# Batch 3's queries and keys by way of DRAM and transposing DMAs, in a fused attention and maxout FFN kernel

## The chip, the cores and the metric

One core of a Trainium2 chip runs the whole program. The metric is the device time of one execution in microseconds; lower is better. The profile's engines are PE (TensorE matmul), PEld (its weight loads), DVE (VectorE), ACT (ScalarE), POOL (GpSimd) and SP (SyncE, which here only issues DMAs).

## The reference

Causal attention over 8 batches of 8 heads, 576 positions, head size 64, with 16 extra "beacon" keys and values ahead of each head's own, followed by a feed-forward layer with three input matrices and a maximum. Shapes: q, k, v are 8 x 8 x 576 x 64 in float32, the beacons 8 x 8 x 16 x 64, the input matrices 512 x 768, the output matrix 768 x 512, the output 4608 x 512.

```python
k_all = concat([beacon_k, k], axis=2); v_all = concat([beacon_v, v], axis=2)
scores = (1 / sqrt(D)) * q @ k_all.T            # a query sees all beacons
scores = where(causal, -1e9, scores)            # and the keys up to its own
a = softmax(scores)
x = (a @ v_all) with the heads side by side      # 4608 tokens x 512
h = max(max(x @ w1, x @ w2), x @ w3)
out = h @ w_out
```

## The kernel before

**The work.** The kernel goes over 32 pairs of heads, four pairs to a batch (`PPB`), in order. For pair p it needs the queries and keys in bf16 with the head dimension on the partitions: one of four tiles `qT` and one of four tiles `kT` (`NT = 4`, so pair p uses the tiles that pair p - 4 used). A burst (`emit_burst`, L505, matmuls at L496) makes the scores of the pair and ACT turns them into exponentials (L514); POOL zeroes what the causal mask hides (`emit_masks`, L536). After every second pair, the products with the values follow (`emit_pv_whole`, L594, matmuls at L613) for the two pairs before, and ACT and DVE normalise them into `xT`. Between bursts PE does the feed-forward layer of earlier tokens: units of matmuls at L689 (input matrices) and L737 (output matrix), which DVE and ACT empty from PSUM (L707, L709, L744).

**The order.** It is written out by hand; each engine takes its instructions in program order. Batches 0 and 1 have functions of their own. From pair 8 on, `emit_all` (L1016) runs one step per pair. Step p is: the burst of pair p; if p is even, the products of pairs p - 2 and p - 1; the masks of pair p; some 4 to 6 units of the feed-forward layer; and the jobs of a plan, kept under (p, 0) and (p, 1). The jobs of (p, 0) come after the step's second unit, those of (p, 1) at its end. In this document "step p" is that turn of the loop.

**How queries and keys reach `qT` and `kT`.** Every pair is loaded in float32 from its input into one of eight `st` tiles (`load_pair`, L217, DMAs at L224) and cast to bf16 by POOL (`cast_pair`, L268, casts at L262, one for q and one for k). From there two ways are in use:

- Batches 1 to 3 (pairs 4 to 15): `turn_pair` (L439) makes 12 transposing matmuls of 96 x 96 on PE (L389) into two PSUM banks; DVE copies out the keys (L434) and ACT the queries (L423, by DVE for four pairs); `place_beacons` (L428) puts the beacon keys ahead of the keys by a small ACT copy (L430). In the main loop the turn of pair p + 1 stands behind the first unit of step p.
- Batches 4 to 7 (pairs 16 to 31): `store_pair` (L370) writes the cast pair to a DRAM tensor by two DMAs (L374), `fetch_pair` (L379) reads it back by two transposing DMAs straight into `qT` and `kT` (L381, L382). `open_dram` (L361) first puts the batch's beacon keys into that tensor (L365), out of `bk16`, which POOL casts once for all four batches (the cast that the profile shows at L811) from `bk32`, loaded by `load_beacons` (L336). For pair p these three jobs stand in the plan at steps p - 5, p - 4 and p - 3.

**The queues.** All of these DMAs but the first few and the weights are issued by SP, in program order: loads of pairs and values, stores to DRAM, fetches, and the output (`store_y`, L767, at L769). A fetch waits on SP for the stores that it reads. Loads have no place of their own in the plan. They stand in a list (L819 to L823: batch by batch the four pairs, then the two pieces of the values, and ahead of batch `B_PE`'s the beacons), and each cast of a pair or of values (`C`, L830) emits the next of the list:

```python
    for b in range(2, B):
        if b == B_PE:
            loads.append(L(load_beacons, B_PE, B, bk32))
        loads += load_pairs(b * PPB, (b + 1) * PPB) + load_v_pieces(b)
```

So loads run about eight casts ahead of the cast that uses them. POOL's list is in program order as well: masks, casts of pairs, casts of values (L307).

Of the kernel before, what the change touches and what calls it, by code (L numbers as in the profile page):

```python
# [16 lines left out]
def kernel(  # L17
# [15 lines left out]
    B, H, S, D = q.shape  # L33
# [26 lines left out]
    PPB = H // 2  # L60
# [1 line left out]
    NPAIR = B * PPB  # L62
    RING = 4

    B_PE = 4

# [48 lines left out]
    psum = ctx.enter_context(tc.tile_pool(name="psum", bufs=1, space=PSUM))  # L117
    dram_pool = ctx.enter_context(tc.tile_pool(name="dram", bufs=B - B_PE, space=bass.MemoryType.DRAM))

# [50 lines left out]
    xT = const.tile([128, n_ct, RING * S], BF16, name="xT")  # L170
    NB_PE = Nb * B_PE
    NB_DMA = Nb * (B - B_PE)
    bT = const.tile([128, PPB, NB_PE], BF16, name="bT")
# [4 lines left out]
    bk32 = const.tile([NB_DMA, H, D], FP32, name="bk32")  # L178
    bk16 = const.tile([NB_DMA, H, D], BF16, name="bk16")
# [24 lines left out]
    by_pool = nc.gpsimd.tensor_copy  # L204
# [156 lines left out]
    def open_dram(b):  # L361
        q_dram[b] = dram_pool.tile([PPB, S, 2 * D], BF16, name="q_dram")
        k_dram[b] = dram_pool.tile([PPB, NK, 2 * D], BF16, name="k_dram")
        lo = Nb * (b - B_PE)
        nc.sync.dma_start(  # L365
# [441 lines left out]
    def at_step(p, g, *fns):  # L807
        plan.setdefault((p, g), []).extend(fns)

    def L(fn, *a):  # L810
        return lambda: fn(*a)  # L811

    def load_v_pieces(b):
        return [L(load_v, b, 0), L(load_v, b, 1)]

    def load_pairs(p0, p1):
        return [L(load_pair, p) for p in range(p0, p1)]

    loads = []  # L819
# [5 lines that stand above are left out]
    def next_load(n=1):  # L825
        for _ in range(n):
            if loads:
                loads.pop(0)()

    def C(fn, *a):  # L830
        def run():
            fn(*a)
            next_load()

        return run
# [166 lines left out]
    for b in range(2, B):  # L1002
        p = b * PPB
        at_step(p + 1, 0, C(cast_v, b, 0, by_pool))
        at_step(p + 1, 1, C(cast_v, b, 1, by_pool))
    at_step(B_PE * PPB - 6, 1, L(by_pool, bk16, bk32))
    for b in range(B_PE, B):
        p = b * PPB
        at_step(p - 4, 0, L(open_dram, b))
        for i in range(PPB):  # L1010
            at_step(p + i - 5, 0, C(cast_pair, p + i, by_pool, by_pool))
            at_step(p + i - 4, 0, L(store_pair, p + i))
            at_step(p + i - 3, 0, L(fetch_pair, p + i))
# [79 lines left out]
```

## Time and profile before

| what | value |
|---|---|
| median of 3 runs | 288.34 us (287.20 to 288.65) |
| the profiled execution's own time | 287.94 us |
| its span, first to last instruction | 286.1 us |
| PE busy | 275.1 us, 96% of the span |
| DVE, ACT, POOL busy | 174.5, 159.4, 136.9 us |
| moved by DMA | 50.59 MB |
| pairs 8, 12, 16, 20: burst starts at | 54.2, 83.0, 115.2, 144.3 us |

Reading: what lies around the span is 287.94 - 286.1 = 1.84 us. "Busy" of PE is the time in which a matmul is in flight by the profile's model, so 96% says that PE hardly ever stands still, not that it works at its peak. Times of DMA issues are those at which SP hands a DMA over; the landing is given as the time from issue.

### The profile page before, as it was taken

The numbers are of one execution on the slowest core, as the hardware profiler recorded it, in microseconds if no ns is written. First come the engines' busy times: TensorE is split into PE (matmuls) and PEld (weight loads), VectorE is DVE, ScalarE is ACT, GpSimd is POOL, SyncE is SP. The second block draws the span as 40 slices with busy tenths as digits, with TensorE's granted clock in tenths as the row PEclk, the third lists the DMA queues.
The fourth block names the chain that finished last, engine by engine and source line by source line (L and its number), as shares of the span: only waits on it lengthen the run. The fifth ranks groups of instructions, "written<-read, shape, count | busy, mean of one in ns | idle before, by whom it ended". The sixth has DMA issues, their size and how long they took to land.

```text
span 286.1 us, 7627 instructions
## 1 busy us (share of the span) xinstructions
PE 275.1 (96%) x2990; PEld 157.6 (55%) x3020; DVE 174.5 (61%) x303; ACT 159.4 (56%) x299; POOL 136.9 (48%) x281
## 2 busy tenths in 40 slices
PE   7889999999999999999999999999999999999995
PEld 4456764555555555555456787455555554444442
DVE  3784666563854838373836383648363847885873
ACT  3686685895666585858585857666676640000000
POOL 7272879667249974548364836583436210000000
PEclk9999999999999999999999999999999999999999
DMA  8999999999999999999999999995221003003004
GB/s 153 199 181 237 230 225 205 256 222 256 266 248 247 293 274 249 183 219 244 306 206 196 286 279 199 236 192 127 63 86 65 0 2 124 22 3 147 0 0 147
DMA packets 85315, 50.59 MB, mean 177 GB/s; under 512 B 64416, under 2 KB 80032, under 8 KB 85280
## 3 DMA queue, kind: packets, MB, share of 16 engines
q1 hardware_dynamic: 80672, 45.76, 69.6%
q0 software_dynamic: 4048, 4.03, 8.8%
q8 instruction: 23, 0.38, 0.6%
q10 hardware_dynamic: 560, 0.33, 0.5%
q14 instruction: 12, 0.10, 0.1%
HBM read 35.13 MB, written 14.22 MB: 172 GB/s over the span
## 4 chain that ended last, share of the span: by engine, by line
PE 76%; POOL 5%; issue 1%; DVE 1%; ACT 0%; POOLq 0%
PE acc L689 44%; PE acc L737 14%; PE acc L613 10%; PE acc L496 6%; POOL p L262 2%; POOL at_sb L536 2%; PE acc L389 1%; POOL v_sb L307 1%; PE acc L755 0%; DVE hT L707 0%; DVE qT L423 0%; ACT at_sb L514 0%; DVE y L762 0%; DVE y L744 0%; POOLq L262 0%
## 5 line engine op out<-in xcount | busy, mean ns | idle before, releaser
L689 PE MATMUL acc<-xT,w_sb 128*128 128x512 bf16 (+4 forms) x721 | 134.1, 337 | 1.2
L707 DVE TENSOR_TENSOR hT<-hT,acc 128x512 bf16<-128x512 bf16 x102 | 70.1, 688 | 59.5 <-PE acc L689 54.8
L689 PEld LDWEIGHTS <-w_sb 128*128 128x128 bf16 x744 | 69.2, 98 | 59.7
L536 POOL TENSOR_SCALAR_AFFINE_SELECT at_sb<-at_sb 128x256 bf16<-128x256 bf16 (+2 forms) x176 | 63.1, 379 | 71.1 <-ACT at_sb L514 66.9
L514 ACT ACTIVATE at_sb<-acc 128x208 bf16<-128x208 f32 (+3 forms) x140 | 89.5, 737 | 5.7 <-PE acc L496 4.5
L737 PE MATMUL acc<-w_out_sb,hT 128*128 128x512 bf16 (+2 forms) x241 | 48.0, 347 | 0.3
L262 POOL CAST p<-st 96x768 bf16<-96x768 f32 x56 | 44.6, 821 | 4.1 <-DMA st<-in_q_dram 2.4
L709 ACT CAST hT<-acc 128x352 bf16<-128x352 f32 x18 | 8.1, 452 | 47.9 <-PE acc L689 47.9
L744 DVE COPY y<-acc 128x512 f32<-128x512 f32 (+1 forms) x35 | 22.0, 628 | 20.8 <-PE acc L737 15.6
L737 PEld LDWEIGHTS <-hT 128*128 128x128 bf16 x246 | 22.6, 98 | 21.7 <-DVE hT L707 1.6
L709 DVE CAST hT<-acc 128x512 bf16<-128x512 f32 (+1 forms) x48 | 26.6, 554 | 9.7 <-PE acc L689 9.5
L496 PE MATMUL acc<-qT,kT 64*128 64x208 bf16 (+1 forms) x336 | 27.5, 280 | 1.5 <-DVE hT L728 0.6
L762 ACT COPY y<-acc 128x320 f32<-128x320 f32 x1 | 0.4, 426 | 46.0 <-PE acc L755 46.0
L496 PEld LDWEIGHTS <-kT 64*128 64x128 bf16 x336 | 15.5, 94 | 14.4 <-issue 3.7
L613 PE MATMUL acc<-at_sb,v_sb 128*32 128x512 bf16 (+5 forms) x672 | 23.1, 281 | 0.3 <-POOL v_sb L307 0.3
L636 DVE TENSOR_TENSOR xT<-raw,recip 128x576 bf16<-128x576 f32 x28 | 22.2, 834 | 0.0
L613 PEld LDWEIGHTS <-v_sb 128*32 128x32 bf16 (+1 forms) x672 | 14.7, 96 | 7.2 <-POOL v_sb L307 0.7
L307 POOL CAST v_sb<-st 128x1536 bf16<-128x1536 f32 (+2 forms) x21 | 18.3, 893 | 0.0
L623 ACT COPY raw<-acc 128x512 f32<-128x512 f32 x28 | 15.8, 637 | 4.5 <-PE acc L613 4.3
L613 PE MATMUL acc<-at_sb,ones 128*32 128x512 bf16 (+4 forms) x336 | 15.5, 284 | 0.1
L490 ACT ACTIVATE at_sb<-acc 128x1024 bf16<-128x1024 f32 (+3 forms) x16 | 13.1, 859 | 3.4 <-PE acc L481 3.4
L434 DVE COPY kT<-acc 128x576 bf16<-128x576 bf16 x12 | 9.0, 752 | 5.9 <-PE acc L389 5.9
(68 smaller groups left out, 172.9 us busy)
## 6 DMA issues: line engine op xcount, KB each, us to landing
out_dram<-y SPq DMA_DIRECT2D x35, 256.0 KB, 3.2
st<-in_q_dram SPq DMA_DIRECT2D x28, 288.0 KB, 5.4
st<-in_k_dram SPq DMA_DIRECT2D x28, 288.0 KB, 5.9
st<-in_v_dram SPq DMA_DIRECT2D x24, 256.0 KB, 5.4
w_sb<-in_moe_w_dram POOLq DMA_DIRECT2D x6, 384.0 KB, 7.0
q_dram<-p SPq DMA_DIRECT2D x16, 144.0 KB, 3.3
k_dram<-p SPq DMA_DIRECT2D x16, 144.0 KB, 3.1
st<-in_v_dram SPq DMA_DIRECT2D x8, 224.0 KB, 6.1
```

The lines of the kernel that those rows point to most:

```text
L262: cast(t16.rearrange("p r h d -> p h r d"), st[0:QP, i * NQ2 : (i + 1) * NQ2].rearrange("p (h r d) -> p h r d", h=2, r=QR),)
L307: cast(v_sb[0:n, t:t1].rearrange("p t h d -> p (t h d)"), st[0:n, (t - t_lo) * H * D : (t1 - t_lo) * H * D],)
L496: nc.tensor.matmul(ps, kTs[p % NT][hs, 128 * t : 128 * t + 128], qTs[p % NT][hs, q0:q1], start=True, stop=True, tile_position=(64 * e, 0),)
L514: nc.scalar.activation(out=both_heads(p, gi)[:, e0:e1], in_=acc[:, first + e0 : first + e1, 0 : g_width(p, gi)], func=AF.Exp, scale=scale,)
L536: nc.gpsimd.affine_select(out=view, in_=view, compare_op=ALU.is_ge, fill=0.0, base=x0, pattern=[[0, 2], [1, hi - lo]], channel_multiplier=-1,)
L613: nc.tensor.matmul(acc[32 * j : 32 * j + 32, bank, lo + q0 - qa : lo + qb - qa], lhsT, at_view(PPQ * quad + j // 2, t, j % 2, q0, qb), sta ...
L636: nc.vector.tensor_mul(xT[:, 2 * g + i, c0 : c0 + S], raw[:, i], recip)
L689: nc.tensor.matmul(ps[:, a:b], w_in[i][:, ct, 128 * ft : 128 * (ft + 1)], xT[:, ct, x0 : x0 + b - a], start=(ct == 0), stop=(ct == n_ct - 1),)
L707: nc.vector.tensor_max(h[:, lo:hi], h[:, lo:hi], ps[:, lo:hi])
L709: (by_act if hi < TOKB else by_dve)(h[:, lo:hi], ps[:, lo:hi])
L737: nc.tensor.matmul(ps[:, lo:hi], hT[:, ft, 128 * tt : 128 * (tt + 1)], w_out_sb[:, ft, lo:hi], start=(ft == 0), stop=(ft == n_ft - 1),)
L744: (by_act if hi < d_model else by_dve)(y[:, lo:hi], ps[:, lo:hi])
```

## The change

`B_PE` goes from 4 to 3, so pairs 12 to 15 go through DRAM instead of being turned on PE. Their jobs are placed more tightly than those of later batches: cast, store and fetch follow each other by half a step and begin at the end of step 9. Everything that depends on `B_PE` follows: the beacons of five batches (not four) are loaded into `bk32`, and that load stands in the list ahead of batch 3's pairs (not ahead of batch 4's); `bT` holds three batches' beacons (not four).

```diff
-    B_PE = 4
+    B_PE = 3
...
-    at_step(B_PE * PPB - 6, 1, L(by_pool, bk16, bk32))
-    for b in range(B_PE, B):
+    at_step(B_PE * PPB - 3, 1, L(by_pool, bk16, bk32))
+    at_step(B_PE * PPB - 2, 0, L(open_dram, B_PE))
+    for i in range(PPB):
+        p = B_PE * PPB + i
+        for n, f in enumerate((C(cast_pair, p, by_pool, by_pool), L(store_pair, p), L(fetch_pair, p))):
+            at_step(*divmod(2 * B_PE * PPB - 5 + i + n, 2), f)
+    for b in range(B_PE + 1, B):
         p = b * PPB
         at_step(p - 4, 0, L(open_dram, b))
         for i in range(PPB):
             at_step(p + i - 5, 0, C(cast_pair, p + i, by_pool, by_pool))
             at_step(p + i - 4, 0, L(store_pair, p + i))
             at_step(p + i - 3, 0, L(fetch_pair, p + i))
```

Written out, the new places are (step, half):

| pair | cast | store | fetch | burst |
|---|---|---|---|---|
| 12 | (9, 1) | (10, 0) | (10, 1) | step 12 |
| 13 | (10, 0) | (10, 1) | (11, 0) | step 13 |
| 14 | (10, 1) | (11, 0) | (11, 1) | step 14 |
| 15 | (11, 0) | (11, 1) | (12, 0) | step 15 |
| 16 (as before) | (11, 0) | (12, 0) | (13, 0) | step 16 |

## The prediction

> **What bounds the kernel now.** First the page's slices, which are also the map of the run:
>
> ```profile
> PE   7889999999999999999999999999999999999995
> POOL 7272879667249974548364836583436210000000
> DMA  8999999999999999999999999995221003003004
> ```
>
> PE is busy from end to end, so what is taken from PE comes off the end. But the DMA row is as full as PE's for the first 27 slices of 7.15 us: until about 195 us transfers stand in line. The change takes work from the first row and puts it into the third, at 65 to 110 us.
>
> Second, the chain that ended last, in order of time. Around pair 12 it is PE, with a turn of 0.51 us in it (12 transposes, L389), and from 83.3 us it runs over POOL:
>
> ```profile
> 78.26 0.51 PE acc L389 x12
> 78.77 4.33 PE acc L689 x24
> 83.10 0.24 PE acc L496 x2
> ...
> 83.97 1.15 POOL at_sb L536 x4
> ```
>
> Third, the busy time by step (a row for each of steps 11, 12, 14, then 16 and 18; the number behind the stretch is its length):
>
> ```profile
> 76.44:83.03 6.59, 6.54 (x52) 3.60 (x53) 5.73 (x9) 4.20 (x9) 0.34 (x1) 1.00 1.01 259
> 83.03:92.08 9.05, 8.74 (x124) 5.23 (x124) 3.15 (x5) 6.86 (x15) 9.05 (x20) 1.00 1.05 253
> 99.59:109.01 9.42, 9.09 (x124) 5.08 (x125) 4.41 (x7) 6.71 (x15) 6.08 (x12) 1.00 1.11 281
> 115.16:122.69 7.53, 7.48 (x110) 4.38 (x111) 2.39 (x4) 6.22 (x13) 3.54 (x8) 1.00 1.02 193
> 129.69:138.08 8.39, 8.34 (x112) 4.64 (x112) 3.77 (x6) 6.08 (x13) 5.07 (x11) 1.00 1.12 251
> ```
>
> Steps 12 and 14 have the work of steps 16 and 18 and one turn more, yet take 1.52 and 1.03 us longer: each holds waiting as well. In step 12 POOL is busy for all 9.05 us. The waits say why:
>
> ```profile
> POOL bk L811 <- DMA bk<-in_beacon_k_dram: 9.1, 1, 9.1
> ```
>
> POOL stood 9.1 us for the beacons (until 82.7 us) with its masks and casts behind.
>
> **What the change removes.** Four turns: 48 transposes with their weight loads on PE, four DVE and four ACT copies (0.75 and 0.65 us), four beacon copies. The copies lie beside PE work; PE is the gain. By pairs of like steps (batch 4 has no turns): step 11 loses its turn, 0.51; step 12 becomes like 16, 9.05 - 7.53 = 1.52; step 13 loses 0.51; step 14 becomes like 18, 9.42 - 8.39 = 1.03. Sum 3.57 us, of which 2.04 are turns (4 x 0.51) and 1.53 waits for POOL. Those waits go because the beacons are now loaded ahead of pair 12, and because casts 12 to 16 spread over steps 9 to 11, where POOL was idle (0.34 us busy of 6.59 in step 11). In step 9 POOL gets more: by the rows of its timeline the masks from 61.0 to 64.4 us, the values 2.6, two pairs 1.6 each and the beacons 0.6, to 70.8, some 3.3 past the step. That delays the masks of pair 10, which no product needs before step 12.
>
> **What it adds: 16 DMAs and a tight date.** Pair 12's burst needs its fetch, and comes at 83.03 - 0.51 = 82.5 us. When does the fetch land? SP's order in the changed kernel is: five beacons, pairs 12, 13, 14, 15, the values of batch 3, outputs between them, pairs 16 and 17, then `open_dram`, **store 12**, pair 18, **fetch 12**. The loads come first because each cast pulls the next load eight casts ahead, while the store comes from a plan job at (10, 0). In the run before, SP reached the same loads here (issues; start, length):
>
> ```profile
> 61.22 0.61 SPq L224 DMA_DIRECT2D st<-in_q_dram  x1
> ...
> 80.35 0.36 SPq L224 DMA_DIRECT2D st<-in_q_dram  x1
> 80.80 0.41 SPq L224 DMA_DIRECT2D st<-in_k_dram  x1
> 81.48 0.31 SPq L224 DMA_DIRECT2D st<-in_q_dram  x1
> 81.85 0.44 SPq L224 DMA_DIRECT2D st<-in_k_dram  x1
> ```
>
> The first is pair 12, the last four are pairs 16 and 17. DMAs issued from 81.4 to 82.3 us took this long to land:
>
> ```profile
> st<-in_q_dram SPq DMA_DIRECT2D x1, 288.0 KB, 5.1
> st<-in_k_dram SPq DMA_DIRECT2D x1, 288.0 KB, 6.0
> ```
>
> So pair 17's keys landed at 81.85 + 6.0 = 87.85 us, and in that stretch the core's 16 DMA engines are busy throughout. The changed kernel sends the same transfers in another order and one 32 KB beacon more, 0.2 us as an estimate (four of them landed over some 0.8 us before 82.7). Pair 17 then lands at about 88.05. The store stands behind it: in the run before, pair 19's keys (issued 87.04, 5.0 to landing), `open_dram` (87.53, 4.7), and store 16 (88.02, 4.5 and 89.70, 3.2) landed at 92.04, 92.23, 92.52 and 92.90, so the three take 0.9 us behind the load ahead. Store 12 lands at 88.95.
>
> Only then may the fetch be issued. The nearest row is a store whose fetch waited for nothing else: keys stored at 118.38, landed 3.0 later (121.4), the key fetch issued at 122.50 behind the query fetch and landed 2.5 later, at 125.0, which is 3.6 us after the store's landing. Fetch 12 lands at 88.95 + 3.6 = 92.5 us. Against 82.5 that is a **stall of 10.0 us** on PE, whose next instruction is the burst; the products, units and bursts behind it wait too.
>
> Are the other fetches late? With the burst of pair 12 at 92.5, step 12 at 7.5 and the slow restart below (2.0), pair 13 is due at 102.0, 14 at 109.0, 15 at 117.4, 16 at 123.6. Store 13 is issued when SP is through with fetch 12 (some 91.1), lands by 94, its fetch by about 97. Store 14 follows at 96, then six loads of values (5.5 us at about 1 us each), and fetch 14 lands by about 104.5: 4.5 us to spare. Fetch 15 lands by about 109, fetch 16 by about 116. All in time. Nothing is paid back later: PE is full behind it.
>
> **The slow restart.** The run before has no pause of PE in mid-run. At its start, after idling, PE ran twelve 320-column matmuls in 3.38 us, then two in 0.45:
>
> ```profile
> 1.52 3.38 PE L449 MATMUL acc<-busy 128*128 128x320 bf16 x12 [1.52 <-DVE busy L182]
> ...
> 6.54 0.45 PE L449 MATMUL acc<-busy 128*128 128x320 bf16 x2
> ```
>
> Without the last one's drain (474 and 299 ns) that is 0.264 us a matmul at first and some 0.15 later; the slow pace holds from 1.5 to about 6.0 us. If the pause brings it back, 4.5 x (1 - 0.15/0.264) = 1.9, say 2.0 us. Bounds 0 (the pace of all later rows) and 2.0; I take 2.0, since the start is the only row that follows a rest. The Trainium skill ("TensorE: Matmul & The Clock Gate", Part 1) says that about 3.4 us without work halve the array's clock and about 3.4 us of work restore it; by its figures the term is an estimated 1.7 and the sum 296.1. The start rows agree with the halving; no row here shows a pause.
>
> **Sum**, on the profiled execution's 287.94 (0.40 under the median of the runs shown): - 3.57 + 10.0 + 2.0 = **296.4 us**.
>
> **Rivals.**
>
> 1. *The clock does not fall in the pause*: 294.4. For: the granted clock is 1.00 in every slice, the slow start included, so this column would not tell. Chance 0.09.
> 2. *The store overtakes the loads in the queue.* SP could issue it at about 83.5; with the shortest landing of any `q_dram` DMA (1.9) it lands at 85.4, the fetch at 89.0: stall 6.5, total 292.9. Against: in the run before the landings above come in the order of issue. The Trainium skill ("DMA: Bandwidth & Descriptors", Queues, rings and completion order) says that completion need not follow the order of issue, though each DMA engine takes its descriptors in ring order. The trace bears out the ring order. Chance 0.05.
> 3. *The fetch is in time, and the kernel is faster.* This decides at one place: store 12 must land before 82.5 - 3.6 = 78.9. Its cast can be done by about 71, and a store lands in 3.3 (median), so were SP and the DMA engines not behind, the fetch would be there by 80. Then only the removal is left: 287.94 - 3.57 = 284.4. Against: pair 16's load was issued at 80.35 though the last cast of batch 2, from which its tile comes free at the latest, was done by 68.6. Chance 0.07.
> 4. *A second fetch is late too.* Fetch 14 behind six loads of values has the least room; half as slow again as I count, with the step before not slowed, eats it and stalls some 3 us: 299.4. Chance 0.08.
>
> That the turns stay is excluded: the changed program has 48 transposes fewer and eight stores and eight fetches more.
>
> **The numbers.** The forecast, pair 12 late and slow restart, has 0.71. Its bounds: the landing 0.9 earlier (loads at 1.06 us each, as pair 12's, which landed at 61.22 + 5.4 and 61.88 + 5.8), the fetch 0.5 quicker and no slow restart give 293.0; a fetch in a full queue (5.7 and 4.7 us to land from 116 to 145 us) adds 2.2, and POOL's waits staying adds 1.5: 300.1. Range 293.0 to 300.0; it takes in rivals 1 and 4 and leaves out 3 and about all of 2. Slower by over 0.5% (what can be told from no change): 0.92; within: 0.01; faster: 0.07.
>
> **What would show it.** In the profile after: PE idle of about 10 us ahead of L496 near 82 us, released by the DMA `kT<-k_dram`; store 12 issued near 83 and landing near 89; fetches issued near 89 and 90; weaker or no waits at L307 and L811; the first matmuls after the pause at about twice their spacing; steps 13 to 15 without pause. Wrong would be no pause (rival 3), a pause under 7 us (the queue is not a line), or a second one ahead of pair 14.

## The result, and the profile after

| | before | after |
|---|---|---|
| median (range), same chip | 288.27 us (287.20 to 288.65) | 299.04 us (297.80 to 300.23) |
| the profiled execution, its span | 287.94, 286.1 us | 300.23, 298.5 us |
| mean granted clock of PE | 1.00 | 0.977 |
| moved by DMA | 50.59 MB | 53.00 MB |

The ratio is 1.036 (95% interval 1.032 to 1.040): 3.6% slower, some 10.8 us by the medians, 12.3 between the two profiled executions. The forecast was 296.4, the range 293.0 to 300.0.

The slices of the page after show the place. PE has two digits of 0 and 4, and the granted clock is 7 and 5 in the same two slices and 8 in the next:

```profile
PE   7799999999904999999998999899999999999995
PEclk9999999999975899999999999999999999999999
DMA  8999999979998987999999979987855001102003
```

DMA is now at 7 or more for the first 29 slices of 7.46 us, to some 216 us; before it was 27 slices of 7.15 us, to some 193.

PE's timeline after, at the bursts of pairs 11, 12 and 13. The bracket holds the wait ahead and what ended it:

```profile
76.18 0.92 PE L496 MATMUL acc<-qT,kT 64*128 64x208 bf16 x12
...
93.81 1.57 PE L496 MATMUL acc<-qT,kT 64*128 64x208 bf16 x12 [11.41 <-DMA kT<-k_dram]
...
103.78 0.90 PE L496 MATMUL acc<-qT,kT 64*128 64x208 bf16 x12
```

PE came to pair 12's burst at 82.39 us and stood 11.41 us. The same twelve matmuls then took 1.57 us, not 0.92.

SP's timeline after says what the fetch stood behind (the last load of pair 17, the beacons, store 12's queries, the last load of pair 18, fetch 12):

```profile
82.49 0.55 SPq L224 DMA_DIRECT2D st<-in_k_dram  x1
83.14 0.40 SPq L365 DMA_DIRECT2D k_dram<-bk  x1
83.63 0.37 SPq L374 DMA_DIRECT2D q_dram<-p  x1
...
86.14 0.34 SPq L224 DMA_DIRECT2D st<-in_k_dram  x1
89.67 1.21 SPq L381 DMA_TRANSPOSE qT<-q_dram  x1
91.00 1.19 SPq L382 DMA_TRANSPOSE kT<-k_dram  x1
```

Pair 12's cast was done at 70.45. SP issued its store at 83.63 and 84.09, behind the loads, as forecast; the store landed at 89.59 and 90.05, behind pair 17's loads (88.44 and 89.19), and the key fetch at 93.76.

The steps by busy time, as before's were shown: steps 12, 14 and 16. Behind the stretch stand its length, the busy time and number of instructions of PE, PEld, DVE, ACT and POOL, PE's granted clock, the busy share of the DMA engines and the GB/s.

```profile
93.81:103.78 9.97, 9.92 (x110) 5.27 (x112) 2.07 (x3) 6.15 (x12) 5.04 (x10) 0.74 1.06 210
110.83:119.22 8.39, 8.34 (x114) 4.64 (x116) 3.61 (x6) 6.08 (x13) 5.01 (x11) 1.00 0.69 205
125.27:132.85 7.58, 7.53 (x112) 4.40 (x112) 2.41 (x5) 6.27 (x13) 4.12 (x9) 1.00 1.15 263
```

Step 14 takes 8.39, as step 18 did before the change. Step 12 has the work of step 16 (7.53 of it busy) and takes 9.97 at a clock of 0.74.

The chain of waits after runs through pair 12's fetch, and then through those of pairs 21, 24 and 25 (the first of the three is shown):

```profile
91.00 2.76 DMA kT<-k_dram
...
155.80 7.21 DMA kT<-k_dram
```

PE's timeline has three waits of that kind behind the first, at pairs 21, 24 and 25:

```profile
163.06 0.88 PE L496 MATMUL acc<-qT,kT 64*128 64x208 bf16 x12 [1.07 <-DMA kT<-k_dram]
...
185.29 0.88 PE L496 MATMUL acc<-qT,kT 64*128 64x208 bf16 x12 [0.49 <-DMA kT<-k_dram]
...
193.62 0.88 PE L496 MATMUL acc<-qT,kT 64*128 64x208 bf16 x12 [0.73 <-DMA kT<-k_dram]
```

**Where the time came from.** Pair 31's burst starts 12.5 us later (225.8 before, 238.3 after). Wait at pair 12 + 11.41, slow step 12 + 2.44 (9.97 - 7.53), later waits + 2.29 (1.07 + 0.49 + 0.73), the turns and their waits - 3.57: + 12.57. The experiments below test each term.

A measure used from here on is the **slack** of a pair: burst start minus the landing of its key fetch, us, read off the trace's events (0.05 means that PE was waiting):

| pair | 12 | 13 | 14 | 15 | 16 | 17 | 18 | 20 | 21 | 24 | 25 | 28 | 31 |
|---|---|---|---|---|---|---|---|---|---|---|---|---|---|
| before | | | | | 11.3 | 9.0 | 8.8 | 7.9 | 8.6 | 8.7 | 8.9 | 12.4 | 20.5 |
| after | 0.05 | 3.8 | 2.5 | 6.4 | 1.1 | 1.1 | 1.2 | 0.4 | 0.05 | 0.05 | 0.05 | 3.9 | 11.9 |

The ratios below leave out executions in a slower state of the chip; the profiled executions of two kernels (stores ahead of fetches, and the last one) were such, so only the order and the places of waits are read from them, not their totals.

PE comes to pair 11's burst between 76.1 and 79.5 us in the profiled executions, though its order up to there is the same in all kernels. A later PE shortens the pause at pair 12 more than it moves the burst behind it (with four tiles for the cast pairs, below, PE came 1.7 us later than after the change, and the burst 0.9). So two kernels are best compared there by the time at which the burst starts.

### The profile page after: what moved, and what is told of

Its sections match the earlier page's. It is cut to its first block, busy times and chain, and to the rows that moved or that the text cites. A ratio compares the mean times of both kernels' runs of the same rounds, so it can differ in the third digit from the quotient of the medians.

```text
span 298.5 us, 7543 instructions
## 1 busy us (share of the span) xinstructions
PE 274.4 (92%) x2942; PEld 156.1 (52%) x2972; DVE 171.3 (57%) x299; ACT 157.0 (53%) x291; POOL 136.8 (46%) x281
## 4 chain that ended last, share of the span: by engine, by line
PE 67%; DMA 11%; SPq 2%; issue 1%; DVE 1%; ACT 1%; POOL 1%; DVEq 0%; POOLq 0%; ACTq 0%
PE acc L689 38%; PE acc L737 13%; PE acc L613 9%; DMA kT<-k_dram 8%; PE acc L496 6%; DMA q_dram<-p 3%; ACT at_sb L514 1%; SPq L381 1%; PE acc L389 1%; SPq L224 1%; DVE hT L707 1%; PE acc L755 0%; POOL v_sb L307 0%; POOL p L262 0%; DVE qT L423 0%
## 5 line engine op out<-in xcount | busy, mean ns | idle before, releaser
L536 POOL TENSOR_SCALAR_AFFINE_SELECT at_sb<-at_sb 128x256 bf16<-128x256 bf16 (+2 forms) x176 | 61.8, 373 | 58.0 <-ACT at_sb L514 53.8
L262 POOL CAST p<-st 96x768 bf16<-96x768 f32 x56 | 45.6, 835 | 39.4 <-DMA q_dram<-p 24.5
L613 PE MATMUL acc<-at_sb,v_sb 128*32 128x512 bf16 (+5 forms) x672 | 24.1, 290 | 0.1
L613 PE MATMUL acc<-at_sb,ones 128*32 128x512 bf16 (+3 forms) x336 | 15.6, 294 | 0.0
L718 PE MATMUL acc<-xT,w_sb 128*128 128x256 bf16 x96 | 11.8, 273 | 0.0
```

The source lines that it names most:

```text
L262: cast(t16.rearrange("p r h d -> p h r d"), st[0:QP, i * NQ2 : (i + 1) * NQ2].rearrange("p (h r d) -> p h r d", h=2, r=QR),)
L536: nc.gpsimd.affine_select(out=view, in_=view, compare_op=ALU.is_ge, fill=0.0, base=x0, pattern=[[0, 2], [1, hi - lo]], channel_multiplier=-1,)
L613: nc.tensor.matmul(acc[32 * j : 32 * j + 32, bank, lo + q0 - qa : lo + qb - qa], lhsT, at_view(PPQ * quad + j // 2, t, j % 2, q0, qb), sta ...
```

## The experiments

**Theory**: SP hands over its DMAs one by one, in program order. Pair 12's fetch is late because its store stands behind loads, and the restart is slow because the array's clock fell in the pause; what is lost there is added to the rest. **Rivals**: the whole line of transfers is what is late, and a wait taken away at one pair comes back at another; or the cause is POOL, its tiles or the bytes. Ratios are to the kernel before on the same chip, with 95% intervals.

### Loads held back

The loads of pairs 16 and 17 and the values are no longer ahead of store 12:

```diff
+    loads[11:15] = loads[13:15] + loads[11:13]
...
-        at_step(p - 2, 1, C(cast_pair, p, by_pool, by_pool))
+        c = L if p == B_PE * PPB - 1 else C
+        at_step(p - 2, 1, c(cast_pair, p, by_pool, by_pool))
...
-        at_step(p + 1, 0, C(cast_v, b, 0, by_pool))
-        at_step(p + 1, 1, C(cast_v, b, 1, by_pool))
+        c = L if b == 2 else C
+        at_step(p + 1, 0, c(cast_v, b, 0, by_pool))
+        at_step(p + 1, 1, c(cast_v, b, 1, by_pool))
...
+    at_step(11, 1, next_load)
+    at_step(12, 1, L(next_load, 2))
+    at_step(13, 1, next_load)
```

(The cast of pair 12, too, pulls no load.)

> The changed kernel, with four loads of the list held back: the casts of step 9 no longer pull loads, pairs 16 and 17 stand ahead of batch 3's values in the list, and the four missing pulls follow in steps 11 to 13. Store 12 and fetch 12 then stand on SP ahead of pairs 16 and 17 and of batch 3's values. The line theory (pair 12's burst waits because its store stands behind loads pulled ahead of it): the wait of 11.4 us ahead of pair 12's burst shrinks to under 1.5, step 12 takes about 7.5 instead of 9.97, and the time falls to 285 to 288. The capacity rival (the 16 DMA engines can't carry the added stores and fetches by then, whatever their order): the wait moves to a later burst and the time stays at 294 to 299.

Measured: 295.92 us, 1.026 (1.022 to 1.030). Pair 12's burst comes at 82.98 without a pause (its keys landed at 82.93, just in time), and step 12 takes 7.53. But its timeline has other waits, of which these are the longest:

```profile
104.33 0.36 PE L613 MATMUL acc<-at_sb,v_sb 128*32 128x208 bf16 x4 [4.33 <-POOL v_sb L307]
...
128.81 0.88 PE L496 MATMUL acc<-qT,kT 64*128 64x208 bf16 x12 [1.16 <-DMA kT<-k_dram]
```

The first is for the values of batch 3. POOL casts the last of them behind pair 18, and its timeline shows that it stands for pair 18's load, which the edit itself put back:

```profile
100.98 0.82 POOL L262 CAST p<-st 96x768 bf16<-96x768 f32 x1 [4.51 <-DMA st<-in_q_dram]
```

A slow stretch follows as well (the clock over 100 to 120 us is 0.83): step 14 takes 16.13 us instead of 8.39. Pairs 24 and 25 wait 0.72 and 0.62. So the loads' place decides pair 12, as the theory says; but 13.9 us taken away there (11.41 + 2.44) made the kernel only some 3 us faster (299.04 - 295.92 = 3.1). That is what the rival expected of the total, but over half of the 13.9 (7.7) came back through the edit's own order, so this run alone does not show the rival right; the kernel with stores ahead of fetches, below, lacks that wait.

### The array kept busy during the pause

```diff
+            if p == B_PE * PPB:
+                fill(free_banks[0], 46)
             emit_burst(p)
```

46 extra matmuls of 512 columns, whose result nobody reads, run ahead of pair 12's burst.

> The changed kernel, with 46 matmuls of 512 columns on PE ahead of pair 12's burst, whose results nothing uses: some 9.9 us of work at the warm pace, inside the wait. The restart theory (the array runs slowly after the pause): step 12 falls from 9.97 to about 7.5 us, pair 12's burst starts at the same time as before within 0.5, and the time falls by 2.4 to about 296.6. The rival (step 12 is slow because it waits for ACT, POOL or PSUM banks): step 12 and the time stay within 0.5.

Measured: 299.38 us, 1.035 (1.031 to 1.038). Its timeline:

```profile
82.15 10.09 PE L397 MATMUL acc<-busy 128*128 128x512 bf16 x46
...
93.99 0.88 PE L496 MATMUL acc<-qT,kT 64*128 64x208 bf16 x12 [1.75 <-DMA kT<-k_dram]
```

After a rest of 1.75 us the burst takes 0.88 and step 12 takes 7.51 at clock 1.00: the pause and nothing else made step 12 slow. Yet the total did not move. Waits at pair 14 (0.97 for the keys, 1.0 for the values) and pair 17 (0.70) appear, and pair 21's burst starts at 163.05, as in the kernel after. The restart is real, and worth nothing here: it is paid to the line of transfers either way.

### The turns taken out and nothing put in

Pairs 12 to 15 are cast and then neither turned nor stored nor fetched; the bursts read what an earlier pair left in the tiles.

```diff
-    at_step(B_PE * PPB - 2, 0, L(open_dram, B_PE))
...
-        for n, f in enumerate((C(cast_pair, p, by_pool, by_pool), L(store_pair, p), L(fetch_pair, p))):
+        for n, f in enumerate((C(cast_pair, p, by_pool, by_pool), L(drop_pair, p))):
```

> The changed kernel without the way through DRAM for pairs 12 to 15: their beacons, stores and fetches are left out (they are cast and then dropped), and their bursts use the queries and keys of the pairs four before. It leaves out part of the computation and shows what the removal of the turns is worth by itself. By the sum: 3.57 us under the kernel before, about 284.7. If the waits for POOL in steps 12 and 14 were not the beacons' doing, only the turns go, 2.0 us: about 286.3.

Measured: 286.33 us, 0.991 (0.988 to 0.994). From pair 11's burst to pair 16's it takes 35.22 us (79.50 to 114.72); the kernel before takes 38.79 (76.37 to 115.16). The difference is the 3.57 of the sum. Over the whole run the gain is smaller: 2.5 us by the medians (288.84 - 286.33), 1.9 to 3.6 by the interval, and so nearer to the 286.3 of the second expectation than to 284.7. Against the kernel without it, the trip through DRAM costs some 12.7 us (299.04 - 286.33).

### The kernel before with its beacons loaded early

The prediction gave 1.53 of the 3.57 us to POOL's wait for the beacons. Here they are loaded ahead of pair 12, and cast a step earlier, in the kernel before:

```diff
-        if b == B_PE:
+        if b == B_PE - 1:
...
-    at_step(B_PE * PPB - 6, 1, L(by_pool, bk16, bk32))
+    at_step(B_PE * PPB - 7, 1, L(by_pool, bk16, bk32))
```

> The kernel before with all its turns, where only the beacons of batches 4 to 7 are loaded ahead of pair 12 instead of pair 16 and cast by POOL one step earlier. If the beacons caused the excess of step 12 (1.0 us) and, by the backlog on POOL, that of step 14 (0.5): 1.0 to 1.5 us under the kernel before, 286.8 to 287.3. If POOL was simply crowded by two pairs' casts in steps 11 to 13, under 0.5 us.

Measured: 288.82 us, 1.001 (0.999 to 1.003): no gain. Step 12 takes 9.45 us and step 14 9.43. In its timeline the turn in step 12 waits for the cast that it turns (and its second half 0.34 once more):

```profile
89.09 0.43 PE L389 MATMUL acc<-ident,p 96*128 96x96 bf16 x6 [0.71 <-POOL p L262]
```

POOL's timeline shows what that cast, pair 13's, stood behind. The cast of pair 16 comes first in POOL's order, and now waits for its own load:

```profile
86.24 0.82 POOL L262 CAST p<-st 96x768 bf16<-96x768 f32 x1 [4.12 <-DMA st<-in_q_dram]
```

So with the beacons out of the way POOL waits for the next load in SP's line, until 86.2 us, where it had waited for the beacons until 82.7. The turn's cast is late either way, since it stands on POOL behind a cast that waits for a transfer. Such waits go with the turns, not with the beacons' date.

### One more tile for the cast pairs

In the kernel after, POOL stands for stores that still read the cast tiles, a wait the prediction had overlooked:

```profile
POOL p L262 <- DMA q_dram<-p: 24.5, 9, 9.0
```

```diff
-tc.tile_pool(name="pair", bufs=3)
+tc.tile_pool(name="pair", bufs=4)
```

> The changed kernel with four instead of three bf16 tiles for cast pairs (the pool named pair), so that a cast waits for the store of the pair four before, not three before. If the casts that wait for these tiles (24.5 us of POOL's waits in the profile) hold up the stores behind them and so the later fetches: the waits of POOL for q_dram<-p fall by more than half, pairs 21, 24 and 25 no longer wait, and the time falls by 2 to 3 us to about 296. If the transfers' own line is what is late, the casts wait less but the fetches land as late as before: within 1 us of 299.

Measured: 299.14 us, 1.038 (1.034 to 1.042). The same row:

```profile
POOL p L262 <- DMA q_dram<-p: 6.6, 1, 6.6
```

The wait falls from 24.5 us in nine places to 6.6 in one, and nothing else changes: pair 12 waits 10.54, and pairs 21, 24 and 25 wait 0.82, 0.56 and 0.72. So POOL's waits for its tiles did not set the time.

### Batch 3's stores issued by ACT

```diff
-            nc.sync.dma_start(
+            (nc.scalar if b == B_PE else nc.sync).dma_start(
```

(in `store_pair` and in `open_dram`)

> The changed kernel with batch 3's beacons and the stores of pairs 12 to 15 issued from ACT's queue; loads, fetches and all later stores stay on SP. The store of pair 12 then no longer stands behind the loads of pairs 16 and 17. If the line on SP makes pair 12 late twice over (store behind loads, then the fetch issued only after the store has landed): the fetch is issued near 86.5 instead of 89.7 and pair 12's wait shrinks from 11.4 to about 8. If the transfers as a whole set the end, the total stays within 1.5 us of 299, since pairs 21 to 25 wait instead; if SP's serial waits for the stores set it, 3 us less or more.

Measured: 296.83 us, 1.030 (1.024 to 1.036). Store 12 now lands at 80.9, nine us earlier, but SP still stands at the loads of pairs 17 and 18 before it comes to fetch 12 (key fetch issued 89.33, landed 94.08). PE loses time to ACT, which stands behind a store's wait with the exponentials behind it:

```profile
80.59 7.04 PE L689 MATMUL acc<-xT,w_sb 128*128 128x512 bf16 x27 [2.00 <-ACT at_sb L514]
...
94.13 1.57 PE L496 MATMUL acc<-qT,kT 64*128 64x208 bf16 x12 [6.51 <-DMA kT<-k_dram]
```

Pair 12's burst starts at 94.13, no earlier than in the kernel after (93.81), and step 12 is slow again. All the gain is later: slack at pairs 16, 17, 20, 21, 24 and 25 is 5.0, 4.0, 4.6, 4.5, 3.1 and 3.2 us, and no later burst waits. The 2.2 us by which it beats the kernel after is the size of the three later waits (2.29), though the intervals of the two ratios overlap.

### All stores issued by ACT

As above with `nc.scalar` for all batches that go through DRAM.

> The changed kernel with all stores of cast pairs and of their beacons (batches 3 to 7) issued from ACT's queue. The same bytes and the same number of DMAs, but SP issues nine fewer a batch and no fetch waits on SP behind its own store. If SP's serial issue and waiting is the line that paces the fetches: the fetches of pairs 16 to 27 land 4 us or more ahead of their bursts, and the time is 287 to 292. If the 16 DMA engines are the limit: the slack of these fetches stays at 0 to 5 us, some pairs still wait, and the time is 296 to 300.

Measured: 298.28 us, 1.034 (1.029 to 1.039). Slack from pair 18 to pair 27 is 9 to 15 us, as before the change, and no burst waits for keys after pair 12. But pair 12 still waits 7.32 us (its burst starts at 93.67, as in the kernel after), and ACT's own stream now holds PE:

```profile
135.29 0.38 PE L496 MATMUL acc<-qT,kT 64*128 64x336 bf16 x6 [1.63 <-ACT y L744]
```

With the same bytes pair 24's keys land at 174.9, in the kernel after at 185.2. So the later fetches are late because of what SP has to issue and wait for ahead of them. But taking DMAs from SP did not pay here, since PE waits for the engine that took them.

### Most of the values' bytes taken away

For batches 4 to 7 the values are replaced by six DMAs of 32 KB in the same places, and not cast; their products read an earlier batch's values. The kernel moves 48.93 MB instead of 53.00.

> The changed kernel with the values of batches 4 to 7 neither loaded nor cast: their six DMAs a batch stay on SP but move 32 KB each, 0.2 MB instead of 1.2 MB a batch, and the products of these batches use batch 3's values. It leaves out part of the computation, and takes bytes away without taking DMAs from SP's line. If bytes through the DMA engines are the limit: from pair 18 on the fetches land 4 us or more ahead of their bursts, no pair waits from 20 on, pair 12's wait (whose line has none of these transfers in it) stays within 1 us of 11.4, and the time falls by 2 to 3 us to about 296.5. If the number of DMAs on SP and their waits is the limit: pairs 20 to 25 still wait, within 1 us of 299.

Measured: 300.33 us, 1.041 (1.035 to 1.047). Pairs 21, 24 and 25 wait 0.98, 0.98 and 0.77 us, and their key fetches take 6.6, 5.6 and 6.8 us from issue to landing (7.2, 5.8 and 6.8 in the kernel after): the values' bytes are not what makes the fetches late. The run says less of SP's issues than it was meant to. SP's issues fall to 22.9 of 29.1 us in the batch from pair 16 on, but in its timeline the four small DMAs of the first piece take up 4.82 us:

```profile
129.22 4.82 SPq L279 DMA_DIRECT2D st<-in_beacon_v_dram  x4
```

The fourth writes where the first wrote and stands for its landing, 3.1 to 4.1 us in three of the four batches. The edit gave back on SP what it had freed.

### Stores ahead of fetches

Where a store and a fetch stand in the same place of the plan, the store goes first, so that SP's wait for one pair doesn't hold the next pair's store. Three kernels: the one after, the one with the loads held back, and the one before as a control.

```diff
+            jobs.append((hs[1], 1, L(store_pair, p)))
+            jobs.append((hs[2], 2, L(fetch_pair, p)))
+            c = C
+            jobs.append((hs[0], 3, c(cast_pair, p, by_pool, by_pool)))
+    for h, rank, f in sorted(jobs, key=lambda j: j[:2]):
+        at_step(*divmod(h, 2), f)
```

> The changed kernel with one order changed: within a place of the plan the store of the next pair is issued ahead of the fetch (before: fetch, then store), so that between a pair's store and its fetch SP has a load and another store to issue and needs to wait less for the landing. Same DMAs, same bytes. The theory that SP's serial waits pace the line: the fetches of pairs 17 to 27 land 3 us or more ahead of their bursts, pairs 21, 24 and 25 no longer wait, pair 12's wait stays within 1 us of 11.4 (the loads ahead of its store are the same), and the time falls by 2 to 3 us to about 296.5. If the number of issues on SP or the DMA engines pace it, slack and time stay, within 1 us of 299.

> Both cures together: four loads held back as in e1_order, and stores ahead of fetches as in f1_swap. If two separate causes make the change slow (the loads ahead of store 12, then SP's waits behind each store): pair 12 waits under 1 us, pair 14's products wait under 2 us for batch 3's values (4.3 in e1_order), no slow restart, fetches of pairs 16 to 27 land 3 us ahead, and the time is 285.5 to 290. If the DMA engines cannot carry the added transfers in this stretch: 293 to 297, as e1_order.

> The kernel before (pairs 12 to 15 turned on PE) with stores ahead of fetches in batches 4 to 7, as a control of f1_swap. Its fetches land 8 us or more ahead of their bursts already, so under either theory the time stays within 0.7 us of the kernel before; under the theory of SP's waits the slack of pairs 17 to 26 grows from about 9 us by 2 us or more, under the other it stays.

Measured: 298.42 us, 1.028 (1.025 to 1.032) for the kernel after; 295.98, 1.023 (1.020 to 1.027) with the loads held back; 288.64, 0.998 (0.995 to 1.000) for the control. The first is 0.6 us below the kernel after by the medians; by the ratios it is 0.7%, with intervals that just meet, and in its profile pairs 20, 21, 24 and 25 wait all the same (0.85, 1.50, 0.34 and 0.95). The other two gain nothing. The second is the instructive one: pairs 12 to 15 have 2.7 to 4.8 us of slack and no pause, step 14 does not wait for values, and the pause stands at pair 16, the first of the next batch, with 1.69 us more at pair 21:

```profile
117.66 1.57 PE L496 MATMUL acc<-qT,kT 64*128 64x208 bf16 x12 [3.12 <-DMA kT<-k_dram]
```

Both kernels with the loads held back take 296 us, and pair 31's burst starts at 234.21 and 233.92 us, with their waits in quite different places. That is what a line that is late as a whole looks like.

The control shows one thing more. Its PE came to pair 11's burst 1.7 us later than in the kernel before (78.08, 76.37), POOL cast the beacons at nearly the same time (83.05, 82.69), and step 12 took 8.05 us instead of 9.05, with its turn and with the beacons at their old date. So 1.0 of the 1.53 us beside the turns is a wait for transfers that shrinks when PE is later.

### Loads held back, and later stores on ACT

The first experiment's kernel, with the stores and `open_dram` of batches 4 to 7 on ACT (`nc.scalar if b > B_PE else nc.sync`).

> The kernel with the loads held back (295.9 us), whose stores of pairs 16 to 31 and whose beacons of batches 4 to 7 are issued from ACT's queue, so that SP has some 12 DMAs a batch fewer to issue (4 to 6 us of its 29). Theory that SP's serial issues carry the delay to the end: the waits for fetches at pairs 14, 17, 21, 24 and 25, together 2.9 us in that kernel, go, and every later key fetch lands 3 us or more ahead of its burst; the product of pair 14's step still waits about 4 us for the values of batch 3, with its slow restart of about 2. That gives 295.9 - 2.9 = 293.0, up to 294.5 if ACT's own waiting costs as it did with batch 3's stores. Rival, that something else (the DMA engines, or PE and POOL themselves) sets the pace from pair 16 on: the waits come back elsewhere and the time stays at 295.5 to 297.

Measured: 299.99 us, 1.033 (1.028 to 1.038). A miss for both sides: above the 295.9 (1.026) that it should have improved, though the intervals touch. SP now stands for stores that ACT issues late, by its own waits (in the kernel with the loads held back the same row has 5.9 us in six places, at most 2.5):

```profile
SPq L381 <- DMA q_dram<-p: 10.5, 3, 5.0
```

and PE stands for ACT and for a fetch:

```profile
94.81 0.38 PE L496 MATMUL acc<-qT,kT 64*128 64x336 bf16 x6 [2.33 <-ACT y L744]
...
120.65 1.57 PE L496 MATMUL acc<-qT,kT 64*128 64x208 bf16 x12 [3.05 <-DMA kT<-k_dram]
```

The Trainium skill ("Trainium Kernel Development and Optimization", Key Constraints) says that issuing from several engines only saves the sequencer's issue time. This run agrees, and here even that saving was small: between the bursts of pairs 16 and 20 SP spends 25.4 us on issuing, in the kernel after 26.0. Ten transposing DMAs took 15.6 us of it, where the kernel after needs 1.25 each. And ACT, which issues the stores, now makes PE wait.

## Why the prediction was right, and where it was not

The forecast was slower for the reason given, and the time lies in the range, near its upper end. Point by point:

- **Pair 12's fetch stands behind loads: right.** Store 12 was issued at 83.63 (forecast near 83), landed at 90.05 (88.95), and its key fetch landed 3.7 us after that (3.6). The wait is 11.41, not 10.0: the term was 1.4 too small, most of it (1.1) in the landing of the store. The experiment with the loads held back shows that it is the place in SP's order that makes pair 12 wait. Rivals 2 (the store overtakes) and 3 (in time) did not happen: the store landed behind the loads ahead of it.
- **The slow restart: right, and a little larger.** 2.44 us, not 2.0, as step 12's 9.97 against step 16's 7.53; with the array kept busy it is gone. So rival 1 fell. The Trainium skill ("TensorE: Matmul & The Clock Gate", Part 1) has the rule that an idle array loses half its clock until it has worked for a while, from which the prediction worked out an estimate of 1.7; the trace agrees with the mechanism and lies above that figure. Contrary to rival 1's remark, the granted clock does show it (0.74 over the step).
- **The turns: right in size for the execution shown, half wrong in reason.** Without the trip, 3.57 us go between pairs 11 and 16; by the medians 2.5 us go in all. The 1.53 beside the turns are not a matter of the beacons' date: moved early in the kernel before, they gain nothing (1.001), since POOL then stands for pair 16's load instead, with the turn's cast behind it. And 1.0 of them depends on when PE gets there, as the control shows.
- **"All in time. Nothing is paid back later": this step failed.** Fetches 13 to 16 were forecast to land by 97, 104.5, 109 and 116; they landed at 99.97, 108.33, 112.79 and 124.22, pair 16's 8.2 us late. That was still ahead of their bursts, but only just for pair 16, and three later bursts waited 2.29 us. Rival 4 had the kind right and the place wrong: pair 14 had 2.5 us to spare. I had compared pairs 12 to 16 with their bursts and taken the kernel before's ease for granted from pair 17 on. In fact pair 16's keys landed 20.4 us later than before (103.83, 124.22), and PE was only 10.2 later (115.16, 125.31): the 11.3 us of slack paid the rest.

Why did SP not catch up? In the kernel before SP spends 26.3 of the 29.1 us of a batch (115.16 to 144.23) on issuing 35 DMAs: eight fetches 10.0, eight stores 3.8, eight loads 5.5, six values 4.9, outputs 1.6, beacons 0.6. The kernel after spends 26.0 of 29.1 and then 28.0 of 30.9. Batch 3's trip adds 17 more DMAs, some 14 us by the same rows (8 x 1.25 + 3.8 + 0.6), and SP has about 3 us a batch to spare. So by this count a delay stays until the loads end. The Trainium skill ("Perfetto Trace Analysis", What "DMA-bound" means) names this case: the kernel can be bound on the issuing engine's sequencer, whose track is then solid with DMAs. SP's 90% agrees with it; and the slack recovered only where stores left SP: batch 3's, all of them, and from pair 22 on in the last kernel (8 us and more), whose PE had by then lost time to ACT as well.

**What stays open.** That SP's issuing itself, not the queue behind it, sets its pace is not isolated: the issue of a DMA is no fixed price (five value DMAs took from 2.8 to 7.7 us), so waiting in the queue may be part of it, and the run meant to free SP's time alone gave it back by a wait of its own. The queue's part can be seen: the key fetches of pairs 21, 24 and 25 landed 7.2, 5.8 and 6.8 us after their issue, where the median is 3.0, and at 3.0 none of the three bursts would have waited. Why they took so long is not shown. Moving stores to ACT always cost ACT as well. What is shown is that the line as a whole is late, that the values' bytes, the cast tiles and the order of stores and fetches are not why, and that fewer stores on SP bring the slack back. A version that takes other DMAs from SP (the outputs) to an engine with idle time was not tried. No version with the change in it beat the kernel before; the best two, with the loads held back, are 2.3% and 2.6% slower (2.0 to 2.7 and 2.2 to 3.0).

## What to carry to other kernels

Before moving work from a full engine to the DMA path, add up the issue times on the queue that will carry it, per stage: here a queue that was issuing for 90% of the time took a one-time delay and kept it. Compare every later consumer's slack with that delay, not only the moved ones'. And take a gain at one wait as a loan until the total moves: here 13.9 us removed at pair 12 were worth 3.1.

## What the runs showed of the hardware

- After 11.41 us of rest the twelve matmuls of a burst took 1.57 us instead of 0.92 and the step 2.44 us more; after 1.75 us of rest they took 0.88. Rests of 3.05, 3.12 and 4.33 us were followed by a slow stretch too (bursts of 1.57 us behind the first two).
- A transposing DMA costs SP about 1.2 us to issue (median 1.21 in the kernel after), a store or load mostly 0.4 to 0.5. The mean over 115 to 186 us was 1.2 to 1.4 in the twelve kernels whose later stores SP issues, and 1.6 in the two in which ACT does.
- SP's DMAs around pair 12 landed in the order of issue, the 288 KB loads of pairs 16 and 17 0.8 to 1.2 us apart (86.13, 87.37, 88.44 and 89.19), then the beacons and store 12 (89.37, 89.59 and 90.05).
- Four more bf16 pairs through DRAM added 2.4 MB in all (50.59 to 53.00), less than 5%, and cost 12.7 us; 4.1 MB taken away elsewhere, in the values, gave nothing back (300.33 us).
